# A projection's second phase waits for VectorE's selection on the scores, one low part is made at once, and half of a phase stands ahead of the scores

## The chip, the core and the metric

The kernel runs on one core of one Trainium2 chip. The metric is the time of one execution in device microseconds; less is better. Of the engines, TensorE (PE in the profile, with PEld for its weight loads) multiplies, VectorE (DVE), ScalarE (ACT) and GpSimd (POOL) work element by element, and SyncE (SP) issues the transfers.

## What is computed

With x of 2048 rows and 512 columns, the output is x + s * g. xn is x normalised by rows. s is attention on xn with 32 heads of 16 columns and a window of 256 rows; g is silu of a two-layer block on xn normalised once more. Cut to what matters:

```python
xn = _layernorm(x)
qkv = (xn @ wqkv)                  # 32 heads of 16 columns, for q, k and v
scores = einsum("bhqd,bhkd->bhqk", q, k) * 16 ** -0.5
mask = (i_q - i_k >= 0) & (i_q - i_k < 256)
s = einsum("bhqk,bhkd->bhqd", softmax(where(mask, scores, -1e9)), v) @ wo
g = silu(gelu(_layernorm(xn) @ w1 + b1) @ w2 + b2)
return x + s * g
```

## The kernel before

Each float32 factor is split into a high part (written by ScalarE or a copy in TensorE's short float format) and a low part (VectorE or GpSimd subtracts the high part from the raw value). A product is three matmul passes: high by high, high by low, low by high. The transposed input xnT lies in SBUF as `big`, high and low, in four slices of 128 columns (kt 0 to 3) and four chunks of 512 rows (c 0 to 3).

The program is written as a list of steps t = -16 to 128, two halves each (the loop ahead of line 900 calls `fill_in(t, 0)` and `fill_in(t, 1)`). Steps below 0 are a ramp: rows are normalised, transposed (`job_x`, L228) and projected to queries and keys (`job_qk(n, c)`: heads of group n, chunk c) and to values (`job_v(hf, i)`), while the score maxima of the first 12 blocks of 128 rows are found (`max_block(0, m)`, L541, with m = t + 12). From step 0 on, the attention proper runs. A table at L798 to L803 says in which half steps a job's matmuls stand; `fills` holds them, and each engine takes its instructions in the order in which the program issues them. VectorE, ScalarE and GpSimd each work strictly in that order too, so a late instruction holds up whatever is behind it.

`max_block` puts the scores of a block into the bank pair `xy` and the oldest third into `zo` (four matmuls each). VectorE then selects between the two under the mask, `COPY_PREDICATED xy<-upper,zo`, and reduces to row maxima, `TENSOR_REDUCE mt<-xy`. The next block's `xy` matmuls wait for that reduction, because they write the same banks.

`by_halves` (L348) runs a projection on two banks. The contraction's 128 rows are cut into an upper and a lower 64, and the two halves of the array work at the same time on different banks: in phase 0 the upper half fills bank 0 and the lower half bank 1, in phase 1 they change banks. A phase is 12 pairs, 24 matmuls. Two halves of the array must not write one bank at once, so phase 1 has to wait until the last pair of phase 0 is through. The kernel before does that with a small GpSimd instruction, `MEMSET sv`, which waits for the last pair (L363) and for which the first pair of phase 1 waits (L367). Jobs come in twos: one on the banks `fb`, one on two banks of the pool `ps_st` (called `pair_-8`, `pair_-5` and `pair_-3` after the step). Their phases alternate, so that one job's phase stands between the other's two.

A job's `finish` has ScalarE write the high part, and VectorE the low part, of a projection (`sh`, then `pjr`), or has ScalarE copy the values into `vt`. The transposes of chunk 3 (`job_x(3)`, step -6) use the banks `fb` for kt 0 and 1 and pool banks (`tr`) for kt 2 and 3. Behind each, ScalarE casts the high part into `xnT` and VectorE subtracts to the low part. `later(k, fn)` issues a step k half steps on; for (c, kt) = (3, 1) the subtraction is put off by one.

The layernorm of chunk 3 is made by ScalarE and GpSimd at step -9 and ends with two `TENSOR_SCALAR x<-x,nm,rss` on GpSimd, issued ahead of the first `MEMSET sv`.

Of the kernel before, what the change touches and what calls it, by code (L numbers as in the profile page):

```python
# [28 lines left out]
ORDER = mybir.DependencyInfo(mybir.DependencyClass.Sync, mybir.DependencyReason.DATA)  # L29
# [21 lines left out]
def mixer_kernel(ctx, tc, x, wqk, wv, wo, w1, b1, w2, b2, out):  # L51


    nc = SimpleNamespace(**{name: Ordered(tc, name) for name in ("tensor", "vector", "scalar", "gpsimd", "sync")})
# [19 lines left out]
    def copy_rows(dst, src):  # L74
        nc.sync.dma_start(dst.bitcast(F32), src.bitcast(F32))
# [102 lines left out]
    zo = psum.tile([P, 2, 512], F32, name="zo")  # L178
    otb = zo[:, 1, 256:384]
    psf = attn.enter_context(tc.tile_pool(name="psf", bufs=1, space=PSUM))  # L180
    fb = [psf.tile([P, 512], F32, name=f"fb{i}") for i in range(2)]
# [5 lines left out]
    def fill_bank():  # L187

        turn[0] ^= 1
        return fb[turn[0]]  # L190
# [29 lines left out]
    mask = upper.bitcast(I32).unsqueeze(1).unsqueeze(1).to_broadcast([P, 2, 2, P])  # L220
    neg = negc.unsqueeze(2).unsqueeze(2).to_broadcast([P, 2, 2, P])
# [6 lines left out]
    def job_x(c):  # L228
        box = []

        def mm(k):
            kt, i = k // 4, k % 4
            if i == 0:
                box.append([fb[0], fb[1], zo[:, 0], None][kt] if c == 1 and kt < 3 or c == 3 and kt < 2 else
                           fill_bank() if c == 2 and kt in (1, 2) else
                           ps_st.tile([P, 512], F32, tag="b", name=f"tr_{c}_{kt}"))
            nc.tensor.transpose(box[kt][:, P * i: P * (i + 1)], xs[c][i][:, P * kt: P * (kt + 1)], ident)
            if i == 3:
                sl = slice(512 * c, 512 * (c + 1))
                nc.scalar.copy(big[:, 0, kt, sl], box[kt])  # L240
                later(int((c, kt) in ((2, 2), (2, 3), (3, 1))),
                      lambda: nc.vector.tensor_sub(big[:, 1, kt, sl], box[kt], big[:, 0, kt, sl].bitcast(F32)))
        return [(109, mm, k) for k in range(16)], lambda: None

# [36 lines left out]
    def later(k, fn):  # L281

        if k == 0:
            fn()
        else:
            h = 2 * now[0] + now[1] + k
            delayed.setdefault((h // 2, h % 2), []).append(fn)

    def job_qk(n, c):

        box = []
        ops = [(kt, a, b) for kt in range(KT) for a, b in PASSES]
        if not n and c < 3:
            ops.sort(key=lambda o: o[2])
        sl = slice(512 * c, 512 * (c + 1))

        def mm(i):
            if i == 0:
                box.append(fill_bank() if c else xy[:, 0])
            kt, a, b = ops[i]  # L300
            nc.tensor.matmul(box[0], wqs[n][:, a, kt], big[:, b, kt, sl],
                             start=(i == 0), stop=(i == len(ops) - 1))

        def half(bank, j, i, r, **flags):
            kt, a, b = ops[i]
            return nc.tensor.matmul(bank[:, 0:256], wqs[n][r, a, kt],
                                    big[r, b, kt, 512 * c + 256 * j: 512 * c + 256 * (j + 1)], **flags)

        def send(src, qk, tt):
            copy_rows(slots[n % 2][tt:P:4, qk, :, sl], src[64 * qk: 64 * qk + 64])  # L310

        def finish():
            hi = sgp.tile([P, 512], F32R, tag="sh", name=f"sh_{n}_{c}", bufs=2)
            raw = t2.tile([P, 512], F32, tag="t2", name=f"pjr_{n}_{c}")
            lo = raw.bitcast(F32R)
            if n:
                for j, bank in enumerate(box):
                    nc.scalar.copy(raw[:, 256 * j: 256 * (j + 1)], bank[:, 0:256])
                box[:] = [raw]
            wide = 512 // len(box)  # L320
            parts = [(bank[:, 0:wide], slice(wide * j, wide * (j + 1))) for j, bank in enumerate(box)]

            def high():
                for src, at_ in parts:
                    nc.scalar.copy(hi[:, at_], src)
                behind(now[0], send_high)

            def send_high():
                for qk, tt in ((1, 0), (0, 0), (1, 2), (0, 1)):
                    send(hi, qk, tt)  # L330

            def low():
                for src, at_ in parts:
                    (nc.gpsimd if n else nc.vector).tensor_tensor(lo[:, at_], src, hi[:, at_].bitcast(F32),
                                                                  op=ALU.subtract)
                behind(now[0], send_low)

            def send_low():
                send(lo, 1, 1)
                send(lo, 0, 2)  # L340

            later(1 if n else 0, high)
            later(3 if n else int(c < 3), low)
        if n or c > 1:
            return half, finish, box
        return [(216, mm, i) for i in range(len(ops))], finish

    def by_halves(job, banks, first, second):  # L348

        half, finish, box = job  # L350
        box[:] = banks
        seen = []
        for phase, where in enumerate((first, second)):
            for i in range(12):
                flags = dict(start=(phase == 0 and i == 0), stop=(phase == 1 and i == 11), skip_group_check=True)

                def unit(i=i, phase=phase, flags=flags):
                    if phase == 0 and i == 0:
                        box[:] = [bank() if callable(bank) else bank for bank in box]
                    two = (half(box[1 - phase], 1 - phase, i, slice(64, P), **flags),  # L360
                           half(box[phase], phase, i, slice(0, 64), **flags))
                    if phase == 0 and i == 11:
                        seen.append(nc.gpsimd.memset(sv[:, 31:32], 0.0))  # L363
                        for r in two:
                            tc.add_manual_dep(seen[0].ins, r.ins.name, ORDER, reason="the rows are through")
                    if phase == 1 and i == 0:
                        for r in two:  # L367
                            tc.add_manual_dep(r.ins, seen[0].ins.name, ORDER, reason="the banks change rows")
                fills.setdefault(where[len(where) * i // 12], []).append((unit, ()))
        fills[second[-1]].append((finish, ()))  # L370

# [169 lines left out]
    def max_block(n, qb, ahead=False):  # L541

        slot = slots[n % 2]
        if qb % 4 == 0:
            mts[n, qb // 4] = small.tile([P, 2, 2, 4], F32, tag="mt", name=f"mt_{n}_{qb}")
        lo = max(qb - 1, 0)
        off = 128 * (lo + 1 - qb)
        for p in range(2):
            for a in (1, 0):
                r = slice(64 * a, 64 * a + 64)  # L550
                nc.tensor.matmul(xy[:, a, 256 * p + off: 256 * (p + 1)], slot[r, 0, p, P * qb: P * (qb + 1)],
                                 slot[r, 1, p, P * lo: P * (qb + 1)], start=True, stop=True)
        if qb >= 2 and not ahead:
            first_scores(n, qb)
        four = xy.rearrange("q a (p k) -> q a p k", p=2)
        nc.vector.copy_predicated(four[:, :, :, 128:256], mask,
                                  neg if qb < 2 else zo[:, :, 0:256].rearrange("q a (p k) -> q a p k", p=2))
        nc.vector.tensor_reduce(out=mts[n, qb // 4][:, :, :, qb % 4],
                                in_=four[:, :, :, off:256],
                                axis=AX.X, op=ALU.max, negate=True)  # L560
# [52 lines left out]
    outs = {}  # L613
# [182 lines left out]
        return ps_st.tile([P, 512], F32, tag="b", name=f"pair_{now[0]}")  # L796

    others = [free_bank, free_bank]  # L798
    for job, banks, first, second in (
            (job_qk(0, 2), fb, [(-8, 0)], [(-7, 0)]), (job_v(0, 4), others, [(-8, 1)], [(-7, 1)]),  # L800
            (job_v(0, 5), fb, [(-5, 0)], [(-4, 0)]), (job_qk(0, 3), others, [(-5, 1)], [(-4, 1)]),
            (job_v(0, 6), fb, [(-3, 0)], [(-2, 0)]), (job_qk(1, 0), others, [(-3, 1)], [(-2, 1)]),
            (job_v(0, 7), fb, [(-1, 0)], [(-1, 1)]), (job_qk(1, 1), fb, [(0, 1), (1, 0)], [(2, 0), (2, 1)])):  # L803
        by_halves(job, banks, first, second)
    fills.update(spread([job_x(3)], [(-6, 0), (-6, 1)]))
    fills[-10, 0][:0] = fills[-11, 1][-5:]
    del fills[-11, 1][-5:]
# [349 lines left out]
    for c in range(2):  # L1157
# [30 lines left out]
        for i in range(NF + 1):  # L1188
# [29 lines left out]
            k = i - o_from  # L1218
# [46 lines left out]
    for g in range(NG + 1):  # L1265
        if g < NG:
# [4 lines left out]
            banks = [(ps_st if k < 2 else ps_yt).tile([P, 512], F32, tag="b", name=f"p_{g}_{k}") for k in range(4)]  # L1271
# [137 lines left out]
```

## Time and profile before

| | |
|---|---|
| median of 3 runs | 742.39 us (741.63 to 743.34) |
| profiled execution, its own time | 741.27 us |
| its span | 739.5 us |
| mean granted TensorE clock | 0.997 |
| TensorE busy | 721.0 us (98%) |
| VectorE / ScalarE / GpSimd busy | 500.4 / 425.7 / 316.9 us |

The span is the stretch from the first to the last instruction in the trace; the execution's own time is 1.77 us more. TensorE has matmuls in flight almost all the time, but overlapping matmuls count as busy, so the share says little on one stretch. The prediction reads the ramp, from about 30 to 69 us, instruction by instruction. A row of the timeline has the start, the duration, the engine, the operation with its tiles and the count, and in brackets how long the engine had been idle and what ended that.

### The profile page before, as it was taken

Reading aid. Unit: us, or ns where it says so; the run is one execution under the profiler, and the core shown is the slowest. Engines: PE = TensorE matmul, PEld = TensorE weight load, DVE = VectorE, ACT = ScalarE, POOL = GpSimd, SP = SyncE. Lnnn points to the kernel's source line nnn. Section 1 sums busy time; section 2 is a strip of 40 time slices with the busy share of each in tenths; the row PEclk is TensorE's granted clock in tenths of the full one; section 3 lists DMA queues with packets and bytes.
Section 4 is the critical chain, followed back from the end, with each engine's and each line's share of the span. In section 5 each row is a group of like instructions: output and inputs, shape, how many; then the busy total and the mean of one; then the engine's idle time right before and its main releaser. Section 6 shows DMA issues by size and latency. Waiting matters only on the chain.

```text
span 739.5 us, 19069 instructions
## 1 busy us (share of the span) xinstructions
PE 721.0 (98%) x7584; PEld 587.6 (79%) x7584; DVE 500.4 (68%) x738; ACT 425.7 (58%) x721; POOL 316.9 (43%) x677
## 2 busy tenths in 40 slices
PE   8979999999999999999999999999999999999997
PEld 7878777777778888777776788888888888888886
DVE  7867677777776676777872666537687855676833
ACT  7727777877777676878877746322344734442001
POOL 7412667777677665777777640113202000001102
PEclk9999999999999999999999999999999999999999
DMA  8324356777767643667714285546313322153701
GB/s 291 80 46 87 79 134 147 210 215 236 208 172 208 184 153 107 150 156 200 218 47 162 80 292 126 201 141 220 109 54 103 104 82 78 66 179 120 245 25 58
DMA packets 61528, 106.77 MB, mean 144 GB/s; under 512 B 12096, under 2 KB 12352, under 8 KB 61440
## 3 DMA queue, kind: packets, MB, share of 16 engines
q1 hardware_dynamic: 61440, 105.56, 48.4%
q8 instruction: 60, 0.98, 0.5%
q14 instruction: 28, 0.23, 0.1%
HBM read 54.53 MB, written 33.82 MB: 119 GB/s over the span
## 4 chain that ended last, share of the span: by engine, by line
PE 88%; ACT 5%; DVE 2%; DMA 1%; issue 1%; POOL 1%; SPq 0%; ACTq 0%; DVEq 0%; POOLq 0%
PE acc L43 20%; PE fb L43 19%; PE zo L43 13%; PE stb L43 9%; PE p L43 9%; PE s L43 6%; PE h L43 6%; PE xy L43 5%; ACT pt L43 3%; PE pv L43 1%; DMA wvr<-in_wv_dram 1%; DVE xnT L43 1%; ACT qk L43 1%; DMA qk<-pjr 1%; DVE xy L43 0%
## 5 line engine op out<-in xcount | busy, mean ns | idle before, releaser
L43 POOL TENSOR_SCALAR_AFFINE_SELECT pt<-pt 128x256 f32<-128x256 f32 x480 | 192.8, 426 | 100.7 <-ACT pt L43 95.3
L43 ACT ACTIVATE pt<-stb 128x768 f32<-128x768 f32 (+1 forms) x244 | 188.7, 773 | 45.7 <-PE stb L43 39.5
L43 DVE TENSOR_REDUCE mt<-xy 128x4 f32<-128x1024 f32 (+1 forms) x128 | 152.6, 1192 | 4.4
L43 DVE COPY_PREDICATED xy<-upper,zo 128x512 f32<-128x512 int32 x112 | 77.9, 695 | 77.9 <-PE xy L43 65.2
L43 POOL TENSOR_TENSOR xo<-xo,gated 128x512 f32<-128x512 f32 x15 | 19.9, 1330 | 220.5 <-DVE gated L43 219.5
L43 PE MATMUL zo<-pt,vt 128*17 128x128 f32 x2880 | 103.7, 275 | 0.0
L43 PE MATMUL fb<-xnT,wqb 64*128 64x512 f32 (+2 forms) x732 | 99.3, 381 | 2.5 <-POOL sv L43 2.5
L43 PE MATMUL stb<-qk 64*128 64x384 f32 (+1 forms) x488 | 95.2, 384 | 5.6 <-ACT pt L43 4.3
L43 PE MATMUL acc<-w,gh 128*128 128x512 f32 x320 | 98.6, 389 | 0.0
L43 PEld LDWEIGHTS stb<-qk 64*128 64x128 f32 x488 | 45.8, 184 | 49.2 <-ACT pt L43 40.5
L43 PEld LDWEIGHTS zo<-pt,vt 128*17 128x17 f32 x2880 | 67.5, 97 | 15.2 <-issue 4.9
L43 PEld LDWEIGHTS acc<-w,gh 128*128 128x128 f32 x320 | 60.1, 188 | 12.4
L43 PEld LDWEIGHTS fb<-xnT,wqb 64*128 64x128 f32 (+1 forms) x732 | 62.8, 186 | 8.8 <-POOL sv L43 2.7
L43 PE MATMUL acc<-w,gl 128*128 128x512 f32 x160 | 62.4, 390 | 0.2 <-DVE gl L43 0.2
L43 PE MATMUL xy<-qk 64*128 64x256 f32 (+2 forms) x536 | 58.4, 291 | 1.2 <-DVE mt L43 1.1
L43 PEld LDWEIGHTS xy<-qk 64*128 64x128 f32 x536 | 46.7, 186 | 6.6 <-issue 2.5
L43 PE MATMUL p<-xnT 128*128 128x512 f32 x189 | 51.8, 389 | 0.0
L43 ACT COPY oraw<-zo 128x128 f32<-128x128 f32 x108 | 28.7, 266 | 36.9 <-PE zo L43 26.8
L43 ACT ACTIVATE gated<-acc 128x512 f32<-128x512 f32 x16 | 8.7, 596 | 62.4 <-DVE acc L43 62.4
L43 PE MATMUL s<-wos,ohl 128*128 128x512 f32 (+1 forms) x204 | 44.3, 377 | 0.0
L43 PEld LDWEIGHTS s<-wos,ohl 128*128 128x128 f32 x204 | 36.8, 188 | 7.1
L43 PEld LDWEIGHTS p<-xnT 128*128 128x128 f32 x189 | 35.5, 188 | 7.4
(198 smaller groups left out, 1195.9 us busy)
## 6 DMA issues: line engine op xcount, KB each, us to landing
qk<-sh SPq DMA_DIRECT2D x128, 128.0 KB
qk<-pjr SPq DMA_DIRECT2D x64, 128.0 KB
oT_d<-oraw SPq DMA_DIRECT2D x32, 256.0 KB
w_d<-in_w_dram SPq DMA_DIRECT2D x14, 512.0 KB
xt_d<-xnT SPq DMA_DIRECT2D x12, 512.0 KB
x<-in_x_dram SPq DMA_DIRECT2D x16, 256.0 KB
w<-w_d SPq DMA_DIRECT2D x16, 256.0 KB
or<-oT_d SPq DMA_DIRECT2D x16, 256.0 KB
```

The costliest lines, as they stand in the source:

```text
L43: r = issue(*args, **kwargs)
```

## The change

Three things are edited. First, `by_halves` takes `by_max`. Where it is set, there is no `MEMSET sv`: the first pair of phase 1 waits for the most recent `COPY_PREDICATED` of `max_block` instead. That selection waits for the scores, and the scores stand behind phase 0 in TensorE's order. Three jobs get it, all three on `fb`: `job_qk(0, 2)`, `job_v(0, 5)` and `job_v(0, 6)`. The jobs beside them on pool banks, and the last two of the table, keep the `MEMSET`. Second, the first phase of `job_v(0, 4)` is spread over the half steps (-8, 0) and (-8, 1) in place of (-8, 1) alone. Third, the low part (3, 1) of `job_x` is no longer put off.

```diff
-                later(int((c, kt) in ((2, 2), (2, 3), (3, 1))),
+                later(int((c, kt) in ((2, 2), (2, 3))),
                       lambda: nc.vector.tensor_sub(big[:, 1, kt, sl], box[kt], big[:, 0, kt, sl].bitcast(F32)))
...
-    def by_halves(job, banks, first, second):
+    def by_halves(job, banks, first, second, by_max=False):
...
-                    if phase == 0 and i == 11:
+                    if phase == 0 and i == 11 and not by_max:
                         seen.append(nc.gpsimd.memset(sv[:, 31:32], 0.0))
...
                     if phase == 1 and i == 0:
                         for r in two:
-                            tc.add_manual_dep(r.ins, seen[0].ins.name, ORDER, reason="the banks change rows")
+                            tc.add_manual_dep(r.ins, (seen or outs["max"])[0].ins.name, ORDER, reason="the banks change rows")
...
-        nc.vector.copy_predicated(four[:, :, :, 128:256], mask,
-                                  neg if qb < 2 else zo[:, :, 0:256].rearrange("q a (p k) -> q a p k", p=2))
+        outs["max"] = nc.vector.copy_predicated(
+            four[:, :, :, 128:256], mask,
+            neg if qb < 2 else zo[:, :, 0:256].rearrange("q a (p k) -> q a p k", p=2)),
...
-    for job, banks, first, second in (
-            (job_qk(0, 2), fb, [(-8, 0)], [(-7, 0)]), (job_v(0, 4), others, [(-8, 1)], [(-7, 1)]),
-            (job_v(0, 5), fb, [(-5, 0)], [(-4, 0)]), (job_qk(0, 3), others, [(-5, 1)], [(-4, 1)]),
-            (job_v(0, 6), fb, [(-3, 0)], [(-2, 0)]), (job_qk(1, 0), others, [(-3, 1)], [(-2, 1)]),
+    for job, banks, first, second, *by_max in (
+            (job_qk(0, 2), fb, [(-8, 0)], [(-7, 0)], True), (job_v(0, 4), others, [(-8, 0), (-8, 1)], [(-7, 1)]),
+            (job_v(0, 5), fb, [(-5, 0)], [(-4, 0)], True), (job_qk(0, 3), others, [(-5, 1)], [(-4, 1)]),
+            (job_v(0, 6), fb, [(-3, 0)], [(-2, 0)], True), (job_qk(1, 0), others, [(-3, 1)], [(-2, 1)]),
...
-        by_halves(job, banks, first, second)
+        by_halves(job, banks, first, second, *by_max)
```

The order of instructions shows what this moves. The first place is TensorE at step -8, from the end of phase 0 of `job_qk(0, 2)` (`fb<-xnT,wqb`) over the scores of block 4 (`xy`, `zo`) to phase 0 of `job_v(0, 4)` (`pair_-8<-wva,xnT`). Before:

```order
L43 MATMUL fb_112<-xnT,wqb_224 128x256 [waits DVE_49]
L43 MATMUL fb_111<-xnT,wqb_224 128x256
L43 MATMUL xy<-qk_94 128x256 [waits DMAHW4_49,DMAHW3_49,DMAHW5_49,DMAHW2_49,DMAHW6_49,DMAHW1_49,DVE_49]
L43 MATMUL xy<-qk_94 128x256 x3
L43 MATMUL zo<-qk_94 128x128 x4
L43 MATMUL pair_-8_613<-wva,xnT 128x256 [waits PE_49]
L43 MATMUL pair_-8_612<-wva,xnT 128x256 [waits Activation_49]
```

With the change, at the same place, the last pair of the half that was moved, the scores, and the other half:

```order
L43 MATMUL pair_-8_600<-wva,xnT 128x256
L43 MATMUL pair_-8_599<-wva,xnT 128x256
L43 MATMUL xy<-qk_94 128x256 [waits DMAHW4_49,DMAHW3_49,DMAHW5_49,DMAHW2_49,DMAHW6_49,DMAHW1_49,DVE_49]
L43 MATMUL xy<-qk_94 128x256 x3
L43 MATMUL zo<-qk_94 128x128 x4
L43 MATMUL pair_-8_600<-wva,xnT 128x256
L43 MATMUL pair_-8_599<-wva,xnT 128x256
```

Twelve matmuls of `pair_-8` now stand ahead of the scores of block 4, and twelve behind them; before, all 24 stood behind. The second place is TensorE at step -7: the end of that phase 0, and the beginning of phase 1 of `job_qk(0, 2)`. Before:

```order
L43 MATMUL pair_-8_613<-wva,xnT 128x256
L43 MATMUL pair_-8_612<-wva,xnT 128x256
L43 MATMUL fb_111<-xnT,wqb_224 128x256 [waits Pool_49]
L43 MATMUL fb_112<-xnT,wqb_224 128x256
L43 MATMUL fb_111<-xnT,wqb_224 128x256
```

With the change, the same place:

```order
L43 MATMUL pair_-8_600<-wva,xnT 128x256
L43 MATMUL pair_-8_599<-wva,xnT 128x256
L43 MATMUL fb_111<-xnT,wqb_224 128x256 [waits DVE_49]
L43 MATMUL fb_112<-xnT,wqb_224 128x256
L43 MATMUL fb_111<-xnT,wqb_224 128x256
```

The wait has gone from GpSimd to VectorE. Some rows on, phase 1 of `job_v(0, 4)` still waits for GpSimd, before and after. Here with the change:

```order
L43 MATMUL fb_112<-xnT,wqb_224 128x256
L43 MATMUL xy<-qk_94 128x256 [waits DVE_49]
L43 MATMUL xy<-qk_94 128x256 x3
L43 MATMUL zo<-qk_94 128x128 x4
L43 MATMUL pair_-8_599<-wva,xnT 128x256 [waits Pool_49]
L43 MATMUL pair_-8_600<-wva,xnT 128x256
```

The third place is VectorE at step -6, from the low part of `job_qk(0, 2)` (`pjr`) over the low parts of chunk 3 (`xnT`) and the selection and reduction of block 6. Before:

```order
L43 TENSOR_TENSOR pjr_2_664<-fb_112,sh_2_663 128x256 [waits Activation_49]
L43 TENSOR_TENSOR xnT<-fb_111,xnT 128x512 [waits Activation_49]
L43 COPY_PREDICATED xy<-upper,zo 128x4x128 [waits DVE_49,PE_49]
L43 TENSOR_REDUCE mt_4_601<-xy 128x4 [waits DVE_49]
L43 TENSOR_TENSOR xnT<-fb_112,xnT 128x512 [waits Activation_49]
L43 TENSOR_TENSOR xnT<-tr_2_734,xnT 128x512 [waits Activation_49]
L43 TENSOR_TENSOR xnT<-tr_3_741,xnT 128x512 [waits Activation_49]
```

With the change:

```order
L43 TENSOR_TENSOR pjr_2_663<-fb_112,sh_2_662 128x256 [waits Activation_49]
L43 TENSOR_TENSOR xnT<-fb_111,xnT 128x512 [waits Activation_49]
L43 TENSOR_TENSOR xnT<-fb_112,xnT 128x512 [waits Activation_49]
L43 COPY_PREDICATED xy<-upper,zo 128x4x128 [waits DVE_49,PE_49]
L43 TENSOR_REDUCE mt_4_614<-xy 128x4 [waits DVE_49]
L43 TENSOR_TENSOR xnT<-tr_2_733,xnT 128x512 [waits Activation_49]
L43 TENSOR_TENSOR xnT<-tr_3_740,xnT 128x512 [waits Activation_49]
```

The subtraction that reads the second bank of `fb` now stands ahead of the selection of block 6, not behind its reduction. On ScalarE and SyncE nothing moves; GpSimd has three instructions fewer.

## The prediction

> **What bounds the kernel now.** I read the chain of waits first: it lies on TensorE for most of the span, so what matters is where TensorE stands still. Then TensorE's waits between 30 and 69 us, the stretch that the change touches:
>
> ```profile
> PE 88%; ACT 5%; DVE 2%; DMA 1%; issue 1%; POOL 1%; SPq 0%; ACTq 0%; DVEq 0%; POOLq 0%
> ```
>
> ```profile
> PE fb L43 <- POOL sv L43: 2.5, 1, 2.5
> PE fb L43 <- DVE xnT L43: 1.8, 1, 1.8
> PE xy L43 <- DVE mt L43: 0.9, 2, 0.6
> ```
>
> Only 5.2 us of waits stand here; the first row is the one that the change renames. Stretches of 2 us (busy time of PE, PEld, DVE, ACT, POOL, then the granted TensorE clock) show what it costs beside its 2.5 us:
>
> ```profile
> 40.00:42.00 2.00, 0.80 (x12) 0.80 (x14) 0.00 (x0) 0.00 (x0) 1.24 (x4) 1.00 0.04 8
> 42.00:44.00 2.00, 2.00 (x28) 2.00 (x26) 0.26 (x1) 0.65 (x2) 0.00 (x0) 0.67 0.00 0
> 44.00:46.00 2.00, 2.00 (x24) 2.00 (x20) 1.97 (x4) 0.00 (x0) 0.00 (x0) 0.50 0.54 116
> 46.00:48.00 2.00, 2.00 (x21) 1.60 (x20) 0.81 (x3) 1.66 (x4) 0.00 (x0) 0.97 0.90 198
> ```
>
> The clock falls to a half after the wait, for 2 x (0.33 + 0.50 + 0.03) x 2 = 3.44 us. So the price of the wait is the standstill and slow matmuls behind it. The timeline of TensorE and GpSimd around it:
>
> ```profile
> 34.37 1.65 PE L43 MATMUL fb<-xnT,wqb 64*128 64x256 f32 x24
> 36.58 0.51 PE L43 MATMUL xy<-qk 64*128 64x256 f32 x4 [0.57 <-DVE mt L43]
> 37.10 0.33 PE L43 MATMUL pair_-8_613<-wva,xnT 64*128 64x256 f32 x1
> 38.46 0.28 PE L43 MATMUL pair_-8_613<-wva,xnT 64*128 64x256 f32 x1
> 39.58 1.52 POOL L43 TENSOR_SCALAR x<-x,nm,rss 128x512 f32<-128x512 f32 x2
> 41.05 0.25 POOL L43 MEMSET sv<- 128x1 f32 x2
> 41.20 1.75 PE L43 MATMUL fb<-xnT,wqb 64*128 64x256 f32 x24 [2.46 <-POOL sv L43]
> 43.49 0.52 PE L43 MATMUL pair_-8_612<-wva,xnT 64*128 64x256 f32 x1
> 45.95 0.35 PE L43 MATMUL pair_-8_612<-wva,xnT 64*128 64x256 f32 x1
> 46.24 1.09 PE L43 MATMUL fb<-ident,x 128*128 128x128 f32 x8
> ```
>
> The last pair of phase 0 starts at 38.46 and is through at 38.74, but GpSimd is in the layernorm until 41.10, and the marker stands behind it. VectorE was done with the selection of block 4 long before:
>
> ```profile
> 37.30 0.69 DVE L43 COPY_PREDICATED xy<-upper,zo 128x512 f32<-128x512 int32 x1
> 38.03 1.23 DVE L43 TENSOR_REDUCE mt<-xy 128x4 f32<-128x1024 f32 x1
> 43.74 0.70 DVE L43 COPY_PREDICATED xy<-upper,zo 128x512 f32<-128x512 int32 x1 [4.48 <-PE zo L43]
> 44.47 1.23 DVE L43 TENSOR_REDUCE mt<-xy 128x4 f32<-128x1024 f32 x1
> 45.61 0.75 DVE L43 TENSOR_TENSOR pjr<-fb,sh 128x256 fp32r<-128x256 f32 x2
> ```
>
> **The change part by part.** For unhindered durations I take a later stretch at full clock, from the timeline:
>
> ```profile
> 50.75 1.69 PE L43 MATMUL fb<-wva,xnT 64*128 64x256 f32 x24 [1.79 <-DVE xnT L43]
> 52.27 0.40 PE L43 MATMUL xy<-qk 64*128 64x256 f32 x4
> 52.69 0.33 PE L43 MATMUL pair_-5_787<-xnT,wqb 64*128 64x256 f32 x1
> 52.90 0.70 DVE L43 COPY_PREDICATED xy<-upper,zo 128x512 f32<-128x512 int32 x1 [1.00 <-PE zo L43]
> 54.17 1.60 PE L43 MATMUL fb<-wva,xnT 64*128 64x256 f32 x24
> ```
>
> From start to start, a phase of 24 matmuls takes 54.17 - 52.69 = 1.48 us (1.52 for the other), eight score matmuls 52.69 - 52.27 = 0.42, and the selection starts 52.90 - 52.27 = 0.63 after the scores.
>
> *Half a phase sooner.* Phase 0 on `fb` starts at 34.37 and is issued by 35.85. Twelve matmuls of `pair_-8` take 0.74 and end at 36.59. The scores of block 4 could not start before 36.58, since the reduction before them ended only then. So they start at 36.59 as before, the half fills TensorE's idle 0.57 us, and the selection keeps its 37.30 to 37.99. The pool banks of `pair_-8` must be free at 35.85 in place of 37.10: one bank's reader, a ScalarE copy into `vt`, ends at 34.74, and the other's, a VectorE subtraction into `xnT`, is awaited by phase 0 on `fb` itself:
>
> ```profile
> 34.17 0.57 ACT L43 COPY vt<-pv 128x512 f32<-128x512 f32 x1
> ```
>
> The other half follows the scores at 37.11 and is issued by 37.85. Alone the edit is worth little, since what follows would wait for 41.20 anyway; together with the next it takes 0.7 us out of the way.
>
> *Selection in place of marker.* Phase 1 on `fb` waits for 37.99 and, with the 0.05 us that lie between the reduction's end (36.53) and the scores (36.58), starts at 38.05, not 41.20. It is issued by 39.53, and the scores of block 5 by 39.95; their reduction (38.03 + 1.23 = 39.26) is done. Behind them stands phase 1 of `pair_-8`, and this one still waits for a `MEMSET` on GpSimd, behind the same layernorm. Nothing that the change touches makes the layernorm sooner. So the wait moves there: 41.20 again, after 1.25 us of standstill. In the row before, that phase started at 43.49. **Term 1: 43.49 - 41.20 = 2.29 us.** Bounds: nothing, if GpSimd were later by as much as TensorE is sooner (no reason in these rows), and no more than this, since 41.20 is fixed by GpSimd.
>
> *The clock.* Before, phase 1 of `pair_-8` and the gap behind it took 46.24 - 43.49 = 2.75 us at half clock; at full clock 1.48 plus 0.02. **Term 2: 1.25 us**, if the clock stays up. Bounds: 0 and 1.25. I take the upper end. The drop came with 1.9 us of standstill between 39.3 and 42.7 (one 3.4 us length before the fall); the next lengths held at most 1.25 us of the 1.79 above (49.5 to 52.9), with no drop; the change leaves 1.25 (39.95 to 41.20), plus 0.2 at 37.85. The transposes then start at 42.70. VectorE allows that: selection of block 5 at 39.53 + 0.63 = 40.16, reduction 0.73 later (44.47 - 43.74) at 40.89, `pjr` 1.14 later (45.61 - 44.47) at 42.03, the first of the two done at 42.4.
>
> The Trainium skill ("TensorE: Matmul & The Clock Gate", "Why this matters for your kernels") says that only idle gaps of over about 3 us, a whole monitoring window, bring back the half clock. This trace does not agree in size: 2.46 us were enough. By the page's rule the change's 1.25 us would be safe too, which leaves the sum as it stands.
>
> *The low part at once.* From the transposes on:
>
> ```profile
> 46.93 1.07 ACT L43 CAST xnT<-fb 128x512 fp32r<-128x512 f32 x2
> 47.55 0.69 DVE L43 TENSOR_TENSOR xnT<-fb,xnT 128x512 fp32r<-128x512 f32 x1 [1.19 <-ACT xnT L43]
> 48.16 0.68 DVE L43 COPY_PREDICATED xy<-upper,zo 128x512 f32<-128x512 int32 x1
> 48.87 1.23 DVE L43 TENSOR_REDUCE mt<-xy 128x4 f32<-128x1024 f32 x1
> 50.02 0.68 DVE L43 TENSOR_TENSOR xnT<-fb,xnT 128x512 fp32r<-128x512 f32 x1
> 50.61 1.28 DVE L43 TENSOR_TENSOR xnT<-tr,xnT 128x512 fp32r<-128x512 f32 x2
> ```
>
> Before, the second subtraction from `fb` stood behind the reduction and ended at 50.70; `job_v(0, 5)` waited 1.79 us for it. With the change: the first cast some 0.74 after the transposes (ScalarE's two `vt` copies stand ahead) at 43.44, the first subtraction 0.62 later at 44.06, the second 0.60 later at 44.66, done at 45.34, `fb` at 45.39. But VectorE's order now puts the selection behind both: 45.27, the reduction 0.71 later at 45.98 to 47.21, the two subtractions from `tr` at 47.13 and 47.73, done at 48.41. TensorE is through with `fb` at 46.9, waits for the reduction until 47.26, and after the scores (47.68) waits for the `tr` bank until 48.46 before phase 0 of `pair_-5`. Before it started at 52.69. From the transposes that is 5.76 us in place of 6.45. **Term 3: 0.69 us.** The edit removes 1.79 us and gives back 1.10 in two new waits for VectorE. Bounds: 0, if VectorE is a little later still, and 1.79, if it is no bound.
>
> *The other two hand-overs* (`job_v(0, 5)`, `job_v(0, 6)`) bring nothing. TensorE passed from 52.69 to 54.17 without a wait before; with the change the selection of block 7 stands behind the `tr` subtractions, 48.33 to 49.02, and phase 1 is wanted at 49.94. Cover gone, it would cost what the selection is late beyond 0.9 us. At the third, the selection of block 9 ends at 60.52 and phase 1 starts at 61.26, both moved alike:
>
> ```profile
> 59.83 0.69 DVE L43 COPY_PREDICATED xy<-upper,zo 128x512 f32<-128x512 int32 x1
> 61.26 1.60 PE L43 MATMUL fb<-wva,xnT 64*128 64x256 f32 x24
> ```
>
> Three markers less on GpSimd are nothing, as it idles there. No transfer is added or passes another in SP's order.
>
> **Sum.** 2.29 + 1.25 + 0.69 = 4.23 us. Everything behind 52.69 is tied to TensorE's progress and moves along. Span 739.5 - 4.2 = 735.3; the profiled execution's 741.27 - 4.23 = 737.0 us. The median of the runs lies 1.1 above that execution, which gives 738.2. I forecast between the two: 737.6 us.
>
> **The rivals.**
>
> *The clock falls all the same* (15 in 100). The 1.25 us at 41 and some 1.1 us at 47 to 48.5 may suffice. For: one drop after 2.46 us. Against: none after 1.79. Term 2 goes (most of it hidden under VectorE's chain otherwise): 4.23 - 1.25 = 2.98, so 738.3 from the profiled execution, 739.4 from the median.
>
> *Given back* (11 in 100). Work ahead of step 0 could be held by something that does not move, such as the row transfers for block 8 or ScalarE's 1.9 us clears. Then the time is 742 to 742.4. Against: the clears stand in ScalarE's order behind copies that wait for TensorE, and move along; the transfers of `pjr` were issued at 46.38, 9.2 us ahead of the scores of block 8 at 55.61, and both move by about 4. The last row is the first work of step 0:
>
> ```profile
> 46.38 1.17 SPq L43 DMA_DIRECT2D qk<-pjr  x2
> 55.61 0.40 PE L43 MATMUL xy<-qk 64*128 64x256 f32 x4
> 68.01 0.34 PE L43 MATMUL stb<-qk 64*128 64x384 f32 x2
> ```
>
> *Slower* (5 in 100). The clock falls at the new gaps and stays at a half through the ramp, from 48.5 to about 64 (68.01 less 4), where matmuls stand close. A half clock over 15.5 us loses half of them, 7.7, so 741.3 - 4.2 + 7.7 = 744.8. It decides from a half clock of over 11 us, which eats 4.2 + 1.5. Against: the drop seen lasted 3.44 us, with busy matmuls ending it.
>
> The Trainium skill (same page, "Seeing it yourself") tells of a clock that stayed at a quarter for over 50 us; no row here shows such a thing.
>
> *The low part undoes nothing* (4 in 100, VectorE not the bound): 2.29 + 1.25 + 1.79 = 5.33, so 735.9.
>
> **How the numbers follow.** My forecast has 65 in 100, the rivals 35. The range of 735.7 to 740.4 takes in the largest sum (735.9) and term 1 alone against the median (742.4 - 2.3 = 740.1), with a few tenths of run to run. About 0.2%, 1.5 us, is what a measurement of this kernel can tell from no change. Forecast, clock and low part are faster by more: 84 in 100; given back is the same: 11; slower: 5.
>
> **What would show it.** Right: the first pair of phase 1 on `fb` starts at about 38.0 behind `COPY_PREDICATED`; TensorE then waits 1.2 us for `sv` ahead of `pair_-8`'s phase 1 at 41.2; the clock stays at 1.00 from 42 to 46; the transposes start at about 42.7, `job_v(0, 5)` at 45.4, `pair_-5` at 48.5 after short waits for `mt` and `xnT`; the first `stb` scores of step 0 about 4.2 us sooner. Wrong: a granted clock near 0.5 after 42 (term 2), `pair_-5` later than 49.2 (term 3), or a step 0 that has not moved.

## The result and the profile after

The changed kernel takes 736.79 us in the median of 4 runs (736.45 to 736.99); the kernel before, in 4 runs, 742.35 us (741.63 to 743.34). The ratio is 0.9924 with a 95% interval of 0.9906 to 0.9941, so 5.56 us less. The profiled execution took 736.99 us with a span of 735.2 us: 4.28 and 4.3 us less than the profiled execution before.

TensorE's waits between 30 and 69 us in the changed kernel, as the waits view gives them (total, times, longest):

```profile
PE pair_-8_599 L43 <- POOL sv L43: 1.1, 1, 1.1
PE xy L43 <- DVE mt L43: 0.5, 2, 0.3
PE stb L43 <- ACT pt L43: 0.3, 1, 0.3
PE pair_-5_784 L43 <- DVE xnT L43: 0.2, 1, 0.2
```

5.2 us of waits have become 2.1, or 1.8 without the wait for `pt`: that one belongs to step 0, which now begins inside this window. The wait for the marker is not gone, it stands ahead of `pair_-8`'s second phase and is 1.1 us long. The wait for the low part (1.8 us) is gone, and two small ones for VectorE have come (0.17 and 0.21 us below). The granted clock in the same stretches of 2 us (the column behind POOL) no longer falls:

```profile
40.00:42.00 2.00, 0.94 (x16) 0.81 (x14) 1.79 (x2) 0.40 (x2) 1.14 (x3) 1.00 0.24 52
42.00:44.00 2.00, 2.00 (x26) 1.70 (x24) 0.79 (x3) 1.08 (x4) 0.00 (x0) 1.00 0.93 199
44.00:46.00 2.00, 2.00 (x24) 1.76 (x26) 1.87 (x3) 1.45 (x4) 0.00 (x0) 1.00 0.66 152
```

The timeline of the changed kernel, from the first hand-over to the first work of step 0:

```profile
37.27 0.70 DVE L43 COPY_PREDICATED xy<-upper,zo 128x512 f32<-128x512 int32 x1
38.02 1.70 PE L43 MATMUL fb<-xnT,wqb 64*128 64x256 f32 x24
41.04 0.10 POOL L43 MEMSET sv<- 128x1 f32 x1
41.19 0.38 PE L43 MATMUL pair_-8_599<-wva,xnT 64*128 64x256 f32 x1 [1.06 <-POOL sv L43]
42.05 0.74 DVE L43 TENSOR_TENSOR pjr<-fb,sh 128x256 fp32r<-128x256 f32 x2
42.82 1.09 PE L43 MATMUL fb<-ident,x 128*128 128x128 f32 x8
45.47 1.70 PE L43 MATMUL fb<-wva,xnT 64*128 64x256 f32 x24
47.34 0.51 PE L43 MATMUL xy<-qk 64*128 64x256 f32 x4 [0.17 <-DVE mt L43]
48.53 0.38 PE L43 MATMUL pair_-5_784<-xnT,wqb 64*128 64x256 f32 x1 [0.21 <-DVE xnT L43]
63.80 0.34 PE L43 MATMUL stb<-qk 64*128 64x384 f32 x2
```

The second phase on `fb` follows VectorE's selection (37.97) by 0.05 us. The transposes of chunk 3 start at 42.82, not 46.24, and the first scores of step 0 at 63.80, not 68.01. These 4.21 us are the gain of the span but for 0.1 us; what follows only moves along.

### The profile page after: what moved, and what is told of

Read it like the earlier page. It is cut to its first block, busy times and chain, and to the rows that moved or that the text cites. A ratio compares the mean times of both kernels' runs of the same rounds, so it can differ in the third digit from the quotient of the medians.

```text
span 735.2 us, 19063 instructions
## 1 busy us (share of the span) xinstructions
PE 720.2 (98%) x7584; PEld 586.3 (80%) x7584; DVE 499.1 (68%) x738; ACT 426.0 (58%) x721; POOL 317.4 (43%) x674
## 4 chain that ended last, share of the span: by engine, by line
PE 90%; ACT 5%; DVE 2%; issue 1%; POOL 1%; DMA 1%; DVEq 0%; ACTq 0%; POOLq 0%
PE acc L43 20%; PE fb L43 19%; PE zo L43 13%; PE stb L43 9%; PE p L43 9%; PE s L43 6%; PE h L43 6%; PE xy L43 5%; ACT pt L43 3%; PE pv L43 1%; ACT x L43 1%; DVE xnT L43 1%; DVE xy L43 0%; ACT xnT L43 0%; DMA x<-in_x_dram 0%
```

## The experiments

The theory: the gain is made in the ramp, out of three things, the release by VectorE, the clock that stays up and the low part at once; the rest of the kernel only moves along. The rivals were that another part of the edit carries it, or that the clock had fallen for another reason. In each execution the mean granted clock over the span tells how much half clock it had: 3.4 us at a half lower the mean by 0.0023. Values of 0.999 and 1.000 are called no stretch below, 0.997 and 0.998 one, 0.995 and 0.996 two. In all 13 profiled executions the clock in stretches of 2 us agrees with this count. Of the other executions only the mean is on record, so behind which standstill a stretch of theirs came is inferred.

### The three waits alone

The half phase and the low part are as before; only `by_max` is taken over. The edit is shown against the changed kernel.

```diff
-            (job_qk(0, 2), fb, [(-8, 0)], [(-7, 0)], True), (job_v(0, 4), others, [(-8, 0), (-8, 1)], [(-7, 1)]),
+            (job_qk(0, 2), fb, [(-8, 0)], [(-7, 0)], True), (job_v(0, 4), others, [(-8, 1)], [(-7, 1)]),
...
-                later(int((c, kt) in ((2, 2), (2, 3))),
+                later(int((c, kt) in ((2, 2), (2, 3), (3, 1))),
```

> The three by_max waits alone: no half phase ahead of the scores, the low part (3, 1) put off as before. Theory A (the gain is the marker's wait passed over, up to the second marker at 41.2 us, and the clock that stays up): phase 1 on fb starts at about 38.6 (behind the 24 matmuls of pair_-8), pair_-8's phase 1 still at 41.2, the clock stays at 1.00, the transposes of chunk 3 start at about 43.0 instead of 46.2, and pair_-5's phase 0 at about 49.4 instead of 52.7: 3.2 us less than before, so about 739.2 us. Rival B (the half phase is what lets VectorE's selection come in time): phase 1 on fb later than 39.5 and less than 2 us gained.

Measured: 739.06 us, ratio 0.9951 (0.9934 to 0.9968), so 3.0 us less than before. Its timeline:

```profile
38.52 1.60 PE L43 MATMUL fb<-xnT,wqb 64*128 64x256 f32 x24
41.16 0.38 PE L43 MATMUL pair_-8_611<-wva,xnT 64*128 64x256 f32 x1 [0.62 <-POOL sv L43]
42.92 1.09 PE L43 MATMUL fb<-ident,x 128*128 128x128 f32 x8
47.44 1.88 PE L43 MATMUL fb<-wva,xnT 64*128 64x256 f32 x24 [1.79 <-DVE xnT L43]
49.86 0.52 PE L43 MATMUL pair_-5_785<-xnT,wqb 64*128 64x256 f32 x1
```

Theory A holds up to the transposes: 38.5, 41.2 and 42.9 against 38.6, 41.2 and 43.0. Then comes something that neither theory had. `pair_-5` starts at 49.86, not 49.4, and runs slowly. The windows show why:

```profile
46.00:48.00 2.00, 0.56 (x8) 0.56 (x10) 2.00 (x4) 0.83 (x2) 0.00 (x0) 1.00 0.04 8
48.00:50.00 2.00, 2.00 (x30) 2.00 (x28) 0.58 (x1) 0.00 (x0) 0.00 (x0) 0.69 0.00 0
50.00:52.00 2.00, 2.00 (x22) 2.00 (x22) 1.86 (x2) 0.00 (x0) 0.00 (x0) 0.50 0.00 0
```

The clock has fallen behind the standstill of 1.79 us, which did no harm in the execution profiled before. Of six executions two had no stretch of half clock (737.5 and 737.8) and four had one (739.0 to 740.4). So a standstill of 1.79 us brings the half clock in some executions and not in others.

### The low part alone

The kernel before, with the one edit in `job_x`, shown against the kernel before.

```diff
-                later(int((c, kt) in ((2, 2), (2, 3), (3, 1))),
+                later(int((c, kt) in ((2, 2), (2, 3))),
```

> The low part (3, 1) at once, alone. Theory A: the transposes start at 46.2 as before; job_v(0, 5) starts 1.8 us sooner after them, but waits for the reduction of block 6 and for the tr bank give back 1.1, so pair_-5 starts about 0.7 us sooner: about 741.7 us. Rival B: VectorE's order is no bound and the whole 1.8 us stay: 740.6. Rival C: nothing stays, 742.4.

Measured: 740.35 us, ratio 0.9972 (0.9962 to 0.9981), 1.75 us less: B's number, but not by B's mechanism. Its timeline shows the standstill of 2.48 us as before, and behind the transposes the waits of theory A:

```profile
41.29 2.45 PE L43 MATMUL fb<-xnT,wqb 64*128 64x256 f32 x24 [2.48 <-POOL sv L43]
46.87 1.09 PE L43 MATMUL fb<-ident,x 128*128 128x128 f32 x8 [0.47 <-DVE pjr L43]
49.52 1.70 PE L43 MATMUL fb<-wva,xnT 64*128 64x256 f32 x24
51.39 0.50 PE L43 MATMUL xy<-qk 64*128 64x256 f32 x4 [0.16 <-DVE mt L43]
52.58 0.38 PE L43 MATMUL pair_-5_786<-xnT,wqb 64*128 64x256 f32 x1 [0.22 <-DVE xnT L43]
```

From the transposes to `pair_-5` it is 5.71 us (5.76 in the prediction, 6.45 before). What is more than that is the clock. Of 12 executions four had no stretch, in the mean 739.72 us, and eight one; none had two. Before, in the 63 executions that stood beside these experiments on three chips, five had none (median 740.38), 35 one (741.82) and 23 two (743.36). With equal clocks the low part is worth 740.45 - 739.72 = 0.73 us (means of the five and the four executions without a stretch), as forecast. The other 1 us goes with the stretches: none of the 12 had a second one, and the standstill of 1.79 us is gone. The one of 2.48 us alone brought the half clock in eight of 12.

### The half phase alone

The kernel before, with one entry of the table changed (only the entry is shown).

```diff
-(job_v(0, 4), others, [(-8, 1)], [(-7, 1)])
+(job_v(0, 4), others, [(-8, 0), (-8, 1)], [(-7, 1)])
```

> The half phase ahead of the scores, alone; the markers on GpSimd and the put-off low part as before. Theory A: TensorE's idle 0.57 us ahead of the scores of block 4 goes, and the wait for the marker grows from 2.46 to about 3.1 us; phase 1 on fb starts at 41.2 as before: no change, 742.4 us. Rival B: the longer standstill makes the half clock longer or earlier, and the time is 0.5 to 1.5 us more.

Measured: 742.44 us, ratio 1.0000 (0.9988 to 1.0012). The wait for the marker grew as said, and nothing was gained. Nine of the 12 executions had two stretches of half clock (23 of the 63 before), so there may be something to rival B's longer half clock; of its 0.5 to 1.5 us the interval leaves room for 0.9 at most. Its profiled execution has two stretches of half clock, the second behind the 1.79 us:

```profile
40.80 2.22 PE L43 MATMUL fb<-xnT,wqb 64*128 64x256 f32 x24 [3.23 <-POOL sv L43]
50.66 1.90 PE L43 MATMUL fb<-wva,xnT 64*128 64x256 f32 x24 [1.79 <-DVE xnT L43]
```

```profile
42.00:44.00 2.00, 2.00 (x22) 2.00 (x22) 0.20 (x1) 0.65 (x2) 0.00 (x0) 0.50 0.00 0
50.00:52.00 2.00, 1.34 (x22) 1.34 (x24) 1.80 (x4) 0.05 (x1) 0.00 (x0) 0.99 0.01 2
52.00:54.00 2.00, 2.00 (x22) 2.00 (x22) 0.65 (x1) 0.00 (x0) 0.10 (x1) 0.50 0.02 4
```

### by_max at the second and third hand-over only

Everything else is as before; the edit is shown against the changed kernel.

```diff
-            (job_qk(0, 2), fb, [(-8, 0)], [(-7, 0)], True), (job_v(0, 4), others, [(-8, 0), (-8, 1)], [(-7, 1)]),
+            (job_qk(0, 2), fb, [(-8, 0)], [(-7, 0)]), (job_v(0, 4), others, [(-8, 1)], [(-7, 1)]),
...
-                later(int((c, kt) in ((2, 2), (2, 3))),
+                later(int((c, kt) in ((2, 2), (2, 3), (3, 1))),
```

> by_max only for the second and third hand-over (job_v(0, 5) and job_v(0, 6)); everything at steps -8 and -7 as before. Theory A: TensorE did not wait at these two, so nothing changes: 742.4 us within 0.5. Rival B: the markers' release cost something that the trace's rows don't show, and 0.5 to 1.5 us are gained; rival C: the selection is late there and up to 1 us is lost.

Measured: 742.71 us, ratio 1.0001 (0.9990 to 1.0013). No effect that can be told from none, as theory A had it. Two of the three new waits do nothing by themselves.

### The change without the half phase, and without the low part

Each undoes one entry of the table or one line of `job_x` in the changed kernel. First the half phase:

```diff
-(job_v(0, 4), others, [(-8, 0), (-8, 1)], [(-7, 1)])
+(job_v(0, 4), others, [(-8, 1)], [(-7, 1)])
```

> The change without the half phase ahead of the scores (by_max and the low part at once stay). Theory A: phase 1 on fb starts at 38.6 in place of 38.0, still well ahead of the marker at 41.2; what is later is the selection and reduction of block 5 and with them the low part pjr, so that the transposes start at about 43.0 in place of 42.8: 0.2 us more than the change, about 737.0. Rival B: the half phase carries the 0.7 us by which it moves TensorE's work: 737.5.

Measured: 736.97 us, ratio 0.9929 (0.9916 to 0.9942), five executions without a stretch of half clock:

```profile
42.99 1.09 PE L43 MATMUL fb<-ident,x 128*128 128x128 f32 x8
63.97 0.34 PE L43 MATMUL stb<-qk 64*128 64x384 f32 x2
```

The transposes and the scores of step 0 start 0.17 us behind the change, which is theory A. (Counted from the first scores in the window, at 33.87 here and 33.81 with the change, it is 0.11 us.) Then the low part:

```diff
-                later(int((c, kt) in ((2, 2), (2, 3))),
+                later(int((c, kt) in ((2, 2), (2, 3), (3, 1))),
```

> The change with the low part (3, 1) put off again (by_max and the half phase stay). Theory A: the transposes start at 42.8 as with the change, and pair_-5's phase 0 6.45 us later as before, at 49.3 in place of 48.5: 0.7 us more than the change, about 737.5 us. Rival B: with TensorE sooner VectorE is less of a bound and the whole 1.8 us of the old wait come back: 738.6.

Measured: 738.09 us, ratio 0.9946 (0.9931 to 0.9960), 1.3 us above the change. Four of six executions had no stretch (737.35 to 738.23, mean 737.77), two had one (738.96 and 739.08), which neither theory had. The four are 1.0 us above the change; the profiled one of them shows theory A's size, with step 0 starting 0.8 us later:

```profile
47.36 1.70 PE L43 MATMUL fb<-wva,xnT 64*128 64x256 f32 x24 [1.79 <-DVE xnT L43]
64.63 0.34 PE L43 MATMUL stb<-qk 64*128 64x384 f32 x2
```

So the standstill of 1.79 us, met at full clock, brought the half clock in two of six executions here and in four of six above.

### A later marker

Three instructions on GpSimd ahead of the marker make the remaining wait as long as the old one.

```diff
+                        if now[0] == -8:
+                            nc.gpsimd.memset(sv[:, 30:31], 1.0)
+                            for _ in range(2):
+                                nc.gpsimd.tensor_tensor(sv[:, 30:31], sv[:, 30:31], mhalf[:, :1], op=ALU.pow)
                         seen.append(nc.gpsimd.memset(sv[:, 31:32], 0.0))
```

> The change, with three more small instructions on GpSimd (a memset and two powers on one column, about 1.3 us together) ahead of the marker for which pair_-8's phase 1 waits. TensorE's standstill there grows from 1.06 to about 2.4 us, as long as the one before. Theory A (the clock gate goes by standstill): the granted clock falls to a half for some 3.4 us again, and the time is 1.3 us for the wait plus 0.6 to 1.3 for the slow matmuls more than the change: 738.7 to 739.4 us. Rival B (the clock fell for another reason before): only the wait is added, clock 1.00 throughout, 738.1.

Measured: 739.09 us, ratio 0.9957 (0.9944 to 0.9970), 2.3 us above the change. Theory A, with the half clock from about 42.2 on:

```profile
42.45 0.58 PE L43 MATMUL pair_-8_599<-wva,xnT 64*128 64x256 f32 x1 [2.38 <-POOL sv L43]
45.31 1.24 PE L43 MATMUL fb<-ident,x 128*128 128x128 f32 x8
```

```profile
42.00:44.00 2.00, 1.55 (x14) 1.55 (x16) 0.73 (x3) 0.00 (x0) 0.40 (x2) 0.56 0.95 202
44.00:46.00 2.00, 2.00 (x19) 1.78 (x18) 0.00 (x0) 0.58 (x2) 0.00 (x0) 0.58 0.65 152
```

The wait adds 42.45 - 41.19 = 1.26 us, the transposes are 2.49 us later; the 1.23 us between are the half clock. Five of six executions had a stretch of half clock; the one without took 738.24, 1.45 us more than the change.

### TensorE kept busy through the old wait

The kernel before, with seven products of the identity with itself (14 instructions in the trace), whose result nothing reads, ahead of the second phase of `job_qk(0, 2)`.

```diff
+                    if phase == 1 and i == 0 and now[0] == -7 and now[1] == 0:
+                        for _ in range(7):
+                            nc.tensor.matmul(zo[:, 0, 0:P], ident, ident, start=True, stop=True)
                     two = (half(box[1 - phase], 1 - phase, i, slice(64, P), **flags),
```

> The kernel before, with seven throw-away 128x128 matmuls of the identity into zo ahead of phase 1 of job_qk(0, 2): they fill about 2.1 of TensorE's 2.46 us of waiting for the marker and remove no wait. Theory A (the half clock is a price of the standstill): the granted clock stays at 1.00 from 42 to 46, and the transposes start at about 45.6 in place of 46.2, since VectorE's selection, reduction and low part behind the scores of block 5 are then the bound: 0.6 us less, about 741.7 us. Rival B: the whole 1.25 us of my clock term are gained: 741.1. Rival C: no effect on the clock: 742.4.

Measured: 740.67 us, ratio 0.9987 (0.9976 to 0.9997), so 1.4 us less than the 742.04 us of the kernel before beside it, for work that does nothing, and less than any of the three theories had. In the profiled execution the marker's release is where it was, and the clock stays up:

```profile
38.60 1.83 PE L43 MATMUL zo<-ident 128*128 128x128 f32 x14
41.15 1.70 PE L43 MATMUL fb<-xnT,wqb 64*128 64x256 f32 x24 [0.72 <-POOL sv L43]
45.66 1.09 PE L43 MATMUL fb<-ident,x 128*128 128x128 f32 x8 [0.90 <-DVE pjr L43]
50.17 1.69 PE L43 MATMUL fb<-wva,xnT 64*128 64x256 f32 x24 [1.79 <-DVE xnT L43]
67.44 0.34 PE L43 MATMUL stb<-qk 64*128 64x384 f32 x2
```

```profile
42.00:44.00 2.00, 2.00 (x40) 2.00 (x37) 0.68 (x1) 0.65 (x2) 0.00 (x0) 1.00 0.03 8
```

The transposes start at 45.66, as theory A had it, and wait 0.90 us for VectorE's low part. Half clock at this place thus cost only some 0.58 us there (46.24 - 45.66), since at full clock TensorE would have waited for VectorE. Seven of 12 executions had no stretch (mean 740.40, as the 740.45 of the five without one before: the products gain nothing but the clock). Five had one, where the 1.79 us still stand, and were 1.79 us longer in the mean; with the low part alone, where only the first standstill is left, the eight with a stretch were 0.96 us longer than the four without. So the stretch that seems to come behind the second standstill costs more.

### The change again, with a fourth by_max, and without by_max

The first of these kernels is the change as it is.

> The change itself once more, for more executions. Theory A (before, an execution has none, one or two stretches of half clock, after the standstills of 2.46 and 1.79 us; the change leaves no standstill over 1.1 us): granted clock 0.999 or 1.000 in every execution, all within 0.5 us of 736.8. Rival B (the four executions so far missed it by chance): a third of them at a clock of 0.997 to 0.998 and 1.3 us longer.

Measured: 736.70 us (736.01 to 736.82), ratio 0.9928 (0.9915 to 0.9941). All five executions are at a clock of 0.999 or 1.000, as the four before them: theory A, though one execution lies 0.8 us below its 736.8. The next one also lets `pair_-8` wait for the selection:

```diff
-(job_v(0, 4), others, [(-8, 0), (-8, 1)], [(-7, 1)])
+(job_v(0, 4), others, [(-8, 0), (-8, 1)], [(-7, 1)], True)
```

> The change, with by_max for job_v(0, 4) too: phase 1 of pair_-8 waits for the selection of block 5 and not for GpSimd. Theory A: the selection ends at 40.9, so that phase starts at 40.9 in place of 41.2; the transposes are then bound by VectorE's low part pjr, at about 42.5 in place of 42.8: 0.3 us less than the change, 736.5 us. Rival B (GpSimd's layernorm of chunk 3 is the bound in any case, or VectorE is): no gain, 736.8.

Measured: 736.50 us (736.15 to 736.77), ratio 0.9927 (0.9914 to 0.9939), beside the change's 736.70 on the same chip. Five executions each can't tell 0.2 us apart for certain, but the timelines lean to theory A. From the first scores in this window (34.05; 33.81 with the change) to those of step 0 it is 63.79 - 34.05 = 29.74 us, with the change 63.80 - 33.81 = 29.99 and, in its second profile, 63.70 - 33.78 = 29.92:

```profile
34.05 0.50 PE L43 MATMUL xy<-qk 64*128 64x256 f32 x4
41.16 0.38 PE L43 MATMUL pair_-8_599<-wva,xnT 64*128 64x256 f32 x1 [0.80 <-DVE xy L43]
63.79 0.34 PE L43 MATMUL stb<-qk 64*128 64x384 f32 x2
```

It is the fastest of the kernels measured here, by a margin that is inside the spread.

The last has the half phase and the low part at once, and all markers, in the kernel before:

```diff
-(job_v(0, 4), others, [(-8, 1)], [(-7, 1)])
+(job_v(0, 4), others, [(-8, 0), (-8, 1)], [(-7, 1)])
...
-                later(int((c, kt) in ((2, 2), (2, 3), (3, 1))),
+                later(int((c, kt) in ((2, 2), (2, 3))),
```

> The change without by_max: the half phase and the low part at once, with all markers on GpSimd. Theory A: the wait for the marker is 3.2 us long, phase 1 on fb starts at 41.2 and the half clock comes in most executions; what stays is the low part's 0.7 us and one stretch of half clock less in many executions, as with the low part alone: about 740.5 us. Rival B (the parts need one another): less than 0.5 us below before.

Measured: 741.34 us, ratio 0.9989 (0.9978 to 1.0000), 0.8 us slower than the 740.5 of theory A; its interval just touches that of the low part alone (0.9962 to 0.9981). Without its partner the half phase makes the standstill 3.18 us long, and of 12 executions one had no stretch of half clock, six had one and five had two, though the 1.79 us are gone:

```profile
41.30 1.97 PE L43 MATMUL fb<-xnT,wqb 64*128 64x256 f32 x24 [3.18 <-POOL sv L43]
```

The second stretch is what neither theory had. Whether one long standstill sets off two stretches in a row stays open; the profiled execution had one.

## Why the prediction was right, and where its sizes were off

Most steps came within 0.1 us of the trace:

| step | forecast | measured |
|---|---|---|
| second phase on `fb` | 38.05 | 38.02 |
| second phase of `pair_-8` | 41.20 | 41.19 |
| transposes of chunk 3 | 42.70 | 42.82 |
| `job_v(0, 5)` | 45.39 | 45.47 |
| scores of block 7 | 47.26 | 47.34 |
| `pair_-5` | 48.46 | 48.53 |
| gain up to there | 4.23 | 4.16 |
| span | 735.3 | 735.2 |

*Half a phase sooner*, "worth little" alone: right; alone it is worth nothing, in the change 0.1 to 0.2 us.

*Selection in place of marker*: the wait did move to `pair_-8` at 41.2. The later marker moves the end with it, and `by_max` there takes some 0.2 us out in the timelines. *The other two hand-overs*: nothing, shown by themselves.

*Terms 1 and 2* came out in the order in which the prediction added them up. Term 1: `pair_-8`'s second phase starts at 41.19 in place of 43.49, 2.30 us sooner (forecast 2.29). Term 2: from there to the transposes it is 42.82 - 41.19 = 1.63 us in place of 2.75, 1.12 us less (forecast 1.25). The later marker, which brings the half clock back with the release in place, makes it 45.31 - 42.45 = 2.86 us, so the clock is worth 1.23 us there. In the other order the same sum splits otherwise: with TensorE kept busy in the kernel before, the clock alone brings 46.24 - 45.66 = 0.58 us, because the transposes then wait 0.90 us for VectorE's low part, and the release brings the other 45.66 - 42.82 = 2.84. The slow matmuls had covered that wait, which the prediction reckoned for the new order but not for the old. So the price of the half clock depends on what else has been taken away.

*Term 3*, 0.69 us: 0.73 between executions without a stretch of half clock.

*A step that did not hold* is "with no drop" behind the standstill of 1.79 us, and with it the step from the profiled execution to the median. The row was read rightly, but it is one execution: elsewhere the same standstill did bring the half clock. The profile before has one stretch. The median lay 1.1 us above it, and the prediction took half of that along, to 737.6; no row stood behind that half. Of the 63 executions of the kernel before, 23 had a second stretch (median 743.36), and even the 35 with one had a median of 741.82, above the profiled 741.27. The change removes both standstills, and no stretch is left in nine executions. Its median is 736.79, 0.2 us below the profiled execution's sum of 737.0. Between executions without any stretch it brings 740.4 - 736.7 = 3.7 us; the other 1.9 of the median's 5.56 is, by the mean clocks, half clock that no longer comes.

The rivals: no half clock in nine executions of the change, and nothing given back behind step 0. A low part that undoes nothing is out too: 0.17 and 0.21 us of new waits for VectorE stand in the changed kernel. 1.79 us were enough for a half clock in six of 12 executions of the two kernels in which only this standstill was long. The Trainium skill ("TensorE: Matmul & The Clock Gate", "Why this matters for your kernels") advises against idle gaps of over some 3 us between bursts of matmuls; by that rule the 1.79 us would be safe, and here the measurement decides against it. Why one execution drops its clock behind such a standstill and the next does not stays open.

## What to carry to other kernels

A marker instruction on another engine releases no sooner than what stands ahead of it on that engine lets it, here a layernorm that held TensorE for 2.46 us. An instruction that waits for the same thing anyway, on an engine that is on time, can take its place. When one wait goes, roll the next ones forward with the rows' durations, engine by engine: here the wait came back after 1.9 us of work, 1.1 us long, and a low part that was made at once delayed a reduction. One profile is one draw where short standstills stand in a program: compare the mean granted clock of several executions before a median is tied to it.

## What was not expected of the hardware

Executions of the kernel before fell into groups by their mean granted clock, 1.000, about 0.9975 and 0.995, with median times of 740.4, 741.8 and 743.4 us, on each of three chips. In the profiled executions these are no, one or two stretches of some 3.4 us at half clock. Where only one standstill of TensorE was long, 2.4 to 2.5 us brought one in 13 of 18 executions (the later marker and the low part alone), 1.79 us in six of 12 (and in five of 12 with TensorE kept busy through the first wait), and 1.1 us or less in none of 19 (the change, the change without the half phase, and with a fourth `by_max`). Fourteen matmul instructions without a use, put into a wait, made the kernel 1.4 us faster in the median.
